# A state-space mixer and two MLPs on one NeuronCore: decays of the first sub-chunks spread by TensorE, weight bits made by ScalarE

## The chip, the cores and the metric

The kernel runs on one NeuronCore of one Trainium2 chip. The metric is device time of one execution in microseconds (us); a time given for a kernel is the median of its runs. Five engines work in it: TensorE (PE in the profile, its weight loads PEld), VectorE (DVE), ScalarE (ACT), GpSimd (POOL), and SyncE (SP), which here only issues transfers.

## The reference

```
log_a = log(clip(a, 1e-6, 1))                      # a: batch 4, heads 8, sequence 768
for c in chunks:                                   # chunks of 32 in the reference
    cum = cumsum(log_a[c]);  L = exp(cum_i - cum_j) for i >= j
    y[c] = ((C B^T) * L) x + (C state) * exp(cum)
    state = exp(sum log_a) * state + sum_j B_j x_j * exp(cum_last - cum_j)
x = softplus(y w1_in) w1_out                       # 3072 tokens, 256 -> 2048 -> 256
return gelu(x w2_in) w2_out                        # the same sizes, gelu = h * sigmoid(1.702 h)
```

Inputs and output are float32. All weights are stored as 64-bit floats, and the kernel reads them as 64-bit integers.

## The kernel before

The sequence is cut into 6 chunks of 128 steps; a chunk has 4 sub-chunks, one for each batch element, so there are 24 sub-chunks s. Sub-chunks 0 to 3 are the first chunk. The order of the instructions is written out by hand; each engine takes its own instructions in the order of the program.

For each sub-chunk VectorE makes the matrix L of all 8 heads by one scan (`at_scan`, line 234) over `abz`, the clipped decays on all 128 partitions, with `eye8`, eight copies of an identity. `at_cb_early` (line 265) makes C B^T on TensorE in PSUM, from a pool of three buffers (`ps_e`). `at_m` (line 299) multiplies the two on VectorE, in two halves, into L itself. Then come the matmuls of `at_y` (line 320) and `at_u` (line 331); `at_out` splits y into a rounded high part xh (ScalarE, line 347) and the rest xl (VectorE, line 78); `at_state` (line 358) keeps the state. `at_small` (line 243) reads the last column of L on GpSimd before `at_m` may overwrite L.

Decays of sub-chunks 0 and 1 come from the input `a_l` by broadcast transfers of one row to 128 partitions (line 175, 512 KB each); they are clipped, and their first column set to zero, by VectorE (lines 152 and 233). The decays of all sub-chunks also come as 192 rows on 96 partitions (`ac`, line 430). VectorE clips them and they are written to two scratch tensors in DRAM (`scr_z`, `scr_a`), from which the later sub-chunks' broadcasts are read (line 177). The constants `cc` (line 428) hold the identity `eye`.

The weights come in units of 512 64-bit words per partition (`w_load`, line 105, 512 KB, three buffers `wraw`). A unit is made into floats in four steps: `w_scale` (line 117 on ScalarE, line 119 on VectorE) scales the high word read as a float, with the exponent's offset taken away; `w_sign` (line 124) masks the sign in the high word on VectorE; `w_join_hi` (line 129) shifts the scaled value left by 3 and joins the sign; `w_join_lo` (line 134) joins the low word's three top bits. Then `split` makes a rounded high part (ScalarE, line 88) and the rest (line 78 on VectorE, line 81 on GpSimd). There are 8 units of each of the four weight matrices (kinds 1i, 1o, 2i, 2o).

After the first chunk's sub-chunks the main loop runs over 192 steps t (2 MLPs of 6 chunks by 16 column blocks). A step has 6 matmuls of `g1` (line 381) into h, the activation g on ScalarE (line 568), and, two steps later, `g2` (lines 395, or 397 to 399). In the first 14 steps one weight unit of the first MLP is made in each step, 1o in the even steps and 1i in the odd; each 1i unit serves two later steps. Sub-chunk s = 4 + t // 4 goes along with step t, with k = t % 4 choosing its part. The second MLP's weights are made in steps 80 to 107. Two buffers hold the scaled values (`wt`).

Of the kernel before, what the change touches and what calls it, by code (L numbers as in the profile page):

```python
# [9 lines left out]
F32 = mybir.dt.float32  # L10
F32R = mybir.dt.float32r
I64 = mybir.dt.int64
U32 = mybir.dt.uint32
AF = mybir.ActivationFunctionType
ALU = mybir.AluOpType
# [3 lines left out]
T = 128  # L19
# [17 lines left out]
@with_exitstack  # L37
def mixer_two_mlps(ctx: ExitStack, tc: tile.TileContext, pack_p, pack_q, pack_s, pack_x, a_l, a_rows, consts, w1i, w1o, w2i, w2o, out):
    nc = tc.nc
# [16 lines left out]

    eye8 = at1.tile([P, NH * T], F32, name="eye8")
    cc = at1.tile([P, 2 + P], F32, name="cc")
# [62 lines left out]

    def w_sign(kind, q):
        hi = raws[kind, q].bitcast(U32)[:, 1::2]
        nc.vector.tensor_scalar(out=hi, in0=hi, scalar1=0x80000000, scalar2=None, op0=ALU.bitwise_and)
        return hi

    def w_join_hi(t, s):
        tu = t.bitcast(U32)
        nc.vector.scalar_tensor_tensor(out=tu, in0=tu, scalar=3, in1=s, op0=ALU.logical_shift_left, op1=ALU.bitwise_or)  # L129

    def w_join_lo(kind, q, t, dst=None):
        lo = raws.pop((kind, q)).bitcast(U32)[:, 0::2]
        o = (t if dst is None else dst).bitcast(U32)
        nc.vector.scalar_tensor_tensor(  # L134
            out=o, in0=lo, scalar=29, in1=t.bitcast(U32), op0=ALU.logical_shift_right, op1=ALU.bitwise_or
        )
        return t.rearrange("p (a f) -> p a f", a=2)

    def w_join(kind, q, t, s):
        w_join_hi(t, s)  # L140
        return w_join_lo(kind, q, t)

# [8 lines left out]
    def clip(o, i):  # L151
        nc.vector.tensor_scalar(out=o, in0=i, scalar1=1e-6, scalar2=1.0, op0=ALU.max, op1=ALU.min)
# [13 lines left out]
    def at_load_a(s):  # L166
        c, b = divmod(s, NB)
        d = sub.setdefault(s, {})
        d["abz"] = at.tile([P, NH, T], F32, tag="abz", name=f"abz{s}")
        abz = d["abz"].rearrange("p h t -> p (h t)")  # L170
        r0 = s * NH
        if s < 2:
            for g in range(2 - s):
                o = slice(g * TB, (g + 1 + s) * TB)
                nc.sync.dma_start(out=abz[:, o], in_=a_l[s : s + 1, o].to_broadcast([P, (1 + s) * TB]))
        else:
            nc.sync.dma_start(
                out=abz, in_=scr_z[r0 : r0 + NH, :].rearrange("(o h) t -> o (h t)", o=1).to_broadcast([P, NH * T])
            )
        if c > 0:  # L180
            d["ad"] = at.tile([P, 2, T], F32, tag="ad", name=f"ad{s}")
            src = scr_a[r0 : r0 + NH, :].rearrange("(g h) t -> h g t", g=2)
            for h in range(4):
                nc.sync.dma_start(out=d["ad"][rows(s, h)], in_=src[h : h + 1].to_broadcast([32, 2, T]))
# [26 lines left out]
    def at_prep(s):  # L211
# [7 lines left out]
        for j in range(2):  # L219
# [4 lines left out]
            )  # L224

    def at_scan(s, half=0):
        d = sub[s]
        if "L" not in d:
            d["L"] = at.tile([P, NH, T], F32, tag="L", name=f"L{s}", bufs=3)
        h = slice(4 * half, 4 * half + 4) if s == 0 else slice(0, NH)  # L230
        if s < 2:
            clip(d["abz"][:, h], d["abz"][:, h])
            nc.vector.memset(d["abz"][:, h, 0:1], 0.0)
        nc.vector.tensor_tensor_scan(  # L234
            out=d["L"][:, h].rearrange("p h t -> p (h t)"), data0=d["abz"][:, h].rearrange("p h t -> p (h t)"),
            data1=eye8[:, h.start * T : h.stop * T], initial=0.0, op0=ALU.mult, op1=ALU.add,
        )
# [21 lines left out]
    def at_cb_early(s):  # L259
        d = sub[s]  # L260
        for g in range(2):
            d["cb", g] = ps_e.tile([P, 2, 512], F32, tag="e", name=f"cb{s}_{g}")
        for q in range(4):
            r = slice(32 * q, 32 * q + 32)
            nc.tensor.matmul(d["cb", q // 2][:, q % 2, 0 : 2 * T], d["B"][r], d["C"][r], start=True, stop=True)  # L265
        for g in range(2):
            d["cb", g] = d["cb", g][:, :, 0 : 2 * T]
# [156 lines left out]
    with tc.manual_schedule():  # L424
        nc.scalar.preload_act_table_set("softplus")
        ac = [hid.tile([P, TB], F32, tag="g", name=f"ac{i}")[0:96, 0 : 2 * T].rearrange("p (k t) -> p k t", k=2) for i in range(3)]
        at_load_a(0)
        nc.sync.dma_start(out=cc, in_=consts)
        at_load_p(0)
        nc.sync.dma_start(out=ac[0], in_=a_rows.rearrange("(p k) t -> p k t", k=2))  # L430
        at_load_a(1)
        at_load_p(1)
        nc.vector.memset(zr, 0.0)
        for i in range(2):
            nc.gpsimd.memset(bs_t[i][:, :, 1, :], 0.0)
        nc.gpsimd.memset(rhs_bd.bitcast(F32), 0.0)
        eye4 = eye.unsqueeze(1).to_broadcast([P, 4, T])
        nc.vector.tensor_copy(eye8[:, 0:TB].rearrange("p (h t) -> p h t", h=4), eye4)
        nc.scalar.activation(eye8[:, TB:].rearrange("p (h t) -> p h t", h=4), eye4, AF.Copy)
        at_scan(0, 0)  # L440

# [3 lines left out]
        nc.sync.dma_start(out=scr_z.rearrange("(p k) t -> p k t", k=2), in_=ac[2])  # L445
        nc.sync.dma_start(out=scr_a.rearrange("(p k) t -> p k t", k=2), in_=ac[1])
        at_scan(0, 1)
        at_cb_early(0)
        at_cb_early(1)
        w_load(w1i, "1i", 0)  # L450
        at_load_p(2)
        at_load_a(2)
        at_load_p(3)
        at_load_a(3)
        at_load_q(0)
        w_load(w1i, "1i", 1)
        at_load_q(1)
        at_load_a(NB)
# [8 lines left out]
        def at_yu(s):  # L467
            at_y(s)
            at_u(s)
            return at_out(s)  # L470

        at_ms(0)
        at_scan(1)
        at_small(1)
        wt = w_scale("1i", 0, nc.scalar)
        xl_of = at_yu(0)
        at_cb_early(2)
        at_ms(1)
        wi_split(W1, 0, w_join("1i", 0, wt, w_sign("1i", 0)))
        at_scan(2)  # L480
        catch_up(act_later)
        catch_up(vec_later)
        at_small(2)
        xl_of()
        at_state(0)
        xl_of = at_yu(1)
        at_cb_early(3)
        at_ms(2)
        at_scan(3)
        at_small(3)  # L490
        xl_of()
        at_state(1)
        xl_of = at_yu(2)
        at_ms(3)
        at_cb_early(NB)
        at_cb_keep(NB)
        at_cb_early(NB + 1)
        at_cb_keep(NB + 1)
        w_load(w1i, "1i", 2)
# [15 lines left out]
        wt = w_scale("1i", 1, nc.scalar)  # L515
        wi_split(W1, 1, w_join("1i", 1, wt, w_sign("1i", 1)))
        W1_units = [("1o", 0)]
# [17 lines left out]
        for t in range(2 * NT + 2):  # L535
# [7 lines left out]
            if t < len(W1_units):  # L543
                w_sg = w_sign(*W1_units[t])
            if NF < t <= 2 * NT:
# [31 lines left out]
            if t < len(W1_units):  # L577
                w_join_hi(wt, w_sg)
            catch_up(vec_later)
# [22 lines left out]
            if t < len(W1_units):  # L602
                kind, q = W1_units[t]
                if kind == "1o":
                    w_join_lo(kind, q, wt, w1of[:, 2 * q : 2 * q + 2, :].rearrange("p m f -> p (m f)"))
                else:
                    wi_split(W1, q, w_join_lo(kind, q, wt))
                if t + 1 < len(W1_units):
                    wt = w_scale(*W1_units[t + 1], nc.scalar)
                if t + 3 < len(W1_units):  # L610
                    kind, q = W1_units[t + 3]
                    w_load(W_in[kind], kind, q)
# [17 lines left out]
            while halves < due:  # L630
                kind, q = W2_units[halves // 2]
                if halves % 2 == 0:
                    half = scaled.pop((kind, q), None) or w_scale(kind, q, nc.vector), w_sign(kind, q)
                else:
                    dst, spl = (w2[0:2], wi_split) if kind == "2i" else (w2[2:4], wo_split)
                    spl(dst, q, w_join(kind, q, *half), psub)
                    if halves // 2 + 3 < len(W2_units):
                        kind, q = W2_units[halves // 2 + 3]
                        w_load(W_in[kind], kind, q)
                halves += 1  # L640
                u = (halves + 1) // 2
                if t >= NT - 1 and u < len(W2_units) and W2_units[u] not in scaled:
                    scaled[W2_units[u]] = w_scale(*W2_units[u], nc.scalar)
# [5 lines left out]
def _lay_out(x, a, B, C):  # L649
# [26 lines left out]
    a_l = a.reshape(NB, NH, NC, T).transpose(2, 0, 1, 3)  # L676
    return pack_p, pack_q, pack_s, pack_x, a_l.reshape(NSUB, NH * T), a_l.reshape(NSUB * NH, T)

# [25 lines left out]
```

## Time and profile before

| what | value |
|---|---|
| median of 3 runs | 606.38 us (606.22 to 606.43) |
| the profiled execution | 605.88 us, of which 604.1 us span |
| PE busy | 580.9 us, 96% of the span |
| DVE busy | 371.4 us, 61% |
| ACT busy | 286.8 us, 47% |
| POOL busy | 125.5 us, 21% |

Busy shares are means over stages with different limits. In the chain of work that ended last, an engine stands for a stretch when the next piece of the chain waited for it, or came behind it on the same engine. "issue" is time in which the profile shows no wait. The matmuls are pipelined, so PE counts as busy also where the next matmul is late by less than a matmul's length.

### The profile page before, as it was taken

What the parts mean: (1) busy time and instruction counts of PE and PEld (TensorE: products, weight loads), DVE (VectorE), ACT (ScalarE), POOL (GpSimd) and SP (SyncE); (2) the same over time, 40 slices, a digit from 0 to 9 for tenths busy, and PEclk for the clock granted to TensorE, in tenths of its full rate; (3) what the DMA queues carried; (4) which work ended last, traced back from release to release, by engine and by line L of the source; (5) the groups of instructions that cost most, each with busy time, mean ns of one, the idle gap of its engine ahead of it and who ended that gap; (6) DMA issues with size and microseconds to landing.
All of it is one profiled execution on the core that took longest, in us unless ns stands there. A gap on an engine that the chain in (4) does not pass through costs nothing.

```text
span 604.1 us, 8843 instructions
## 1 busy us (share of the span) xinstructions
PE 580.9 (96%) x3424; PEld 460.5 (76%) x3424; DVE 371.4 (61%) x534; ACT 286.8 (47%) x485; POOL 125.5 (21%) x111
## 2 busy tenths in 40 slices
PE   3779999999999999999999999999999999999997
PEld 2445657788888888888888887888888888888885
DVE  5788987998977978787468798223332232232321
ACT  1254424554444443434455876454454544454443
POOL 1011043444634445343021243000000000000000
PEclk9999999999999999999999999999999999999999
DMA  7846654344234342350032340000000000000000
GB/s 244 289 153 217 212 181 146 105 138 153 76 133 141 106 158 84 118 199 7 1 105 73 102 146 29 36 1 1 35 1 0 36 0 2 35 1 0 36 0 36
DMA packets 27001, 53.36 MB, mean 88 GB/s; under 512 B 3120, under 2 KB 8656, under 8 KB 26960
## 3 DMA queue, kind: packets, MB, share of 16 engines
q1 hardware_dynamic: 26960, 52.80, 26.5%
q8 instruction: 27, 0.44, 0.3%
q14 instruction: 14, 0.11, 0.1%
HBM read 49.45 MB, written 3.34 MB: 87 GB/s over the span
## 4 chain that ended last, share of the span: by engine, by line
PE 81%; DVE 13%; issue 3%; ACT 1%; DMA 1%; POOL 0%; SPq 0%; DVEq 0%; POOLq 0%; ACTq 0%
PE h L381 37%; PE o L397 13%; PE o L399 12%; PE o L398 12%; DVE L L234 2%; DVE L L299 2%; PE y L320 2%; PE cb L289 1%; PE o L395 1%; DVE gl L78 1%; DVE wt_1i L129 1%; DMA x<-pack_p 1%; PE y L311 1%; PE cb L265 1%; DVE x L134 1%
## 5 line engine op out<-in xcount | busy, mean ns | idle before, releaser
L78 DVE TENSOR_TENSOR gl<-g,gh 128x512 fp32r<-128x512 f32 x176 | 141.9, 808 | 170.6 <-ACT gh L404 170.3
L568 ACT ACTIVATE g<-h 128x512 f32<-128x512 f32 x192 | 114.7, 598 | 250.8 <-PE h L381 238.5
L404 ACT ACTIVATE gh<-g 128x512 fp32r<-128x512 f32 x176 | 111.3, 632 | 5.6
L381 PE MATMUL h<-xh,w1ih 128*128 128x512 f32 x192 | 80.9, 421 | 0.7 <-ACT cb_1k L279 0.7
L381 PE MATMUL h<-xl,w1ih 128*128 128x512 f32 x192 | 75.9, 395 | 0.0
L399 PE MATMUL o<-gl,w2oh 128*128 128x512 f32 x192 | 74.8, 390 | 0.3 <-DVE gl L78 0.3
L398 PE MATMUL o<-gh,w2oh 128*128 128x512 f32 x192 | 74.7, 389 | 0.0
L381 PE MATMUL h<-x2h,w2ih 128*128 128x512 f32 x192 | 74.7, 389 | 0.0
L381 PE MATMUL h<-x2l,w2ih 128*128 128x512 f32 x192 | 74.7, 389 | 0.0
L397 PE MATMUL o<-gh,w2ol 128*128 128x512 f32 x192 | 74.7, 389 | 0.0
L381 PE MATMUL h<-xh,w1il 128*128 128x512 f32 x192 | 60.2, 395 | 4.6 <-DVE w1il L78 4.6
L234 DVE TENSOR_TENSOR_SCAN L<-abz,eye 128x1024 f32<-128x1024 f32 (+1 forms) x25 | 63.5, 2542 | 0.2
L397 PE MATMUL o<-gh,w1ol 128*128 128x512 f32 x160 | 63.2, 395 | 0.0
L398 PE MATMUL o<-gh,w1oh 128*128 128x512 f32 x160 | 62.4, 390 | 0.0
L399 PE MATMUL o<-gl,w1oh 128*128 128x512 f32 x160 | 62.3, 389 | 0.0
L381 PE MATMUL h<-x2h,w2il 128*128 128x512 f32 x192 | 59.1, 389 | 0.0
L81 POOL TENSOR_TENSOR rhs_bd<-tc,pk 64x512 fp32r<-64x512 f32 x32 | 53.0, 1656 | 1.2
L381 PEld LDWEIGHTS h<-xh,w1il 128*128 128x128 f32 x192 | 36.0, 189 | 14.1 <-DVE w1il L78 6.3
L381 PEld LDWEIGHTS h<-xh,w1ih 128*128 128x128 f32 x192 | 36.4, 190 | 10.4 <-issue 2.6
L381 PEld LDWEIGHTS h<-xl,w1ih 128*128 128x128 f32 x192 | 36.4, 189 | 8.9 <-issue 2.9
L399 PEld LDWEIGHTS o<-gl,w2oh 128*128 128x128 f32 x192 | 36.0, 188 | 8.2 <-DVE gl L78 0.7
L381 PEld LDWEIGHTS h<-x2h,w2il 128*128 128x128 f32 x192 | 36.0, 188 | 7.5
(100 smaller groups left out, 699.6 us busy)
## 6 DMA issues: line engine op xcount, KB each, us to landing
abz<-scr_z SPq DMA_DIRECT2D x22, 512.0 KB, 3.9
pk<-pack_s SPq DMA_DIRECT2D x16, 512.0 KB, 4.4
px<-pack_x SPq DMA_DIRECT2D x20, 320.0 KB, 3.0
wraw_1i<-w1i SPq DMA_DIRECT2D x8, 512.0 KB, 3.7
wraw_1o<-w1o SPq DMA_DIRECT2D x8, 512.0 KB, 3.4
wraw_2i<-w2i SPq DMA_DIRECT2D x8, 512.0 KB, 3.8
wraw_2o<-w2o SPq DMA_DIRECT2D x8, 512.0 KB, 3.3
out<-ot SPq DMA_DIRECT2D x12, 256.0 KB, 2.0
```

Of the source, the lines that this page charges most:

```text
L78: nc.vector.tensor_sub(o, x, y)
L81: nc.gpsimd.tensor_tensor(out=o, in0=x, in1=y, op=ALU.subtract)
L129: nc.vector.scalar_tensor_tensor(out=tu, in0=tu, scalar=3, in1=s, op0=ALU.logical_shift_left, op1=ALU.bitwise_or)
L234: nc.vector.tensor_tensor_scan(out=d["L"][:, h].rearrange("p h t -> p (h t)"), data0=d["abz"][:, h].rearrange("p h t -> p (h t)"), data1=e ...
L299: nc.vector.tensor_mul(m, d["cb", g], m)
L320: nc.tensor.matmul(d["y"][32 * h : 32 * h + 32, g * T : g * T + T], d["x"][:, x0 : x0 + D], d["M", g][:, h, :], start=(s < NB), stop=True, ...
L381: nc.tensor.matmul(h, w[:, k, f], x[:, k, :], start=(n == 0), stop=(n == 5))
L397: nc.tensor.matmul(acc[c][j], wl[:, m, o], d["gh"], start=first, stop=False)
L398: nc.tensor.matmul(acc[c][j], wh[:, m, o], d["gh"], start=False, stop=False)
L399: nc.tensor.matmul(acc[c][j], wh[:, m, o], d["gl"], start=False, stop=last)
L404: nc.scalar.activation(d["gh"], d["g"], AF.Copy)
L568: nc.scalar.activation(d["g"], d["h"], AF.Softplus if t < NT else AF.Gelu_apprx_sigmoid)
```

## The change

Sub-chunks 0 and 1 no longer get their decays by broadcast transfers. The 96-partition tile `ac` is loaded first, clipped, and `at_spread_a` multiplies it on TensorE by a column of the identity that is repeated 128 times, so that the rows of one partition appear on all 128 partitions of a PSUM tile; four matmuls make a sub-chunk. The scan reads that tile. The transfers of the start are put in another order, both halves of `eye8` are made by ScalarE, and the first weight unit is joined after sub-chunk 2's `at_m` instead of before its scan. In every weight unit `w_sign` is replaced by `w_three`: ScalarE reads the top byte of each low word (stride 8 bytes) and writes its three top bits as an integer into the low word; VectorE's two joins stay, the second with the sign mask in it.

```diff
-    def w_sign(kind, q):
-        hi = raws[kind, q].bitcast(U32)[:, 1::2]
-        nc.vector.tensor_scalar(out=hi, in0=hi, scalar1=0x80000000, scalar2=None, op0=ALU.bitwise_and)
-        return hi
-    def w_join_hi(t, s):
+    def w_three(kind, q):
+        raw = raws[kind, q]
+        lo = raw.bitcast(U32)[:, 0::2]
+        nc.scalar.activation(lo, raw.bitcast(U8)[:, 3::8], AF.Copy, scale=1.0 / 32, bias=-31.0 / 64)
+        return lo
+    def w_join_lo(t, lo):
         tu = t.bitcast(U32)
-        nc.vector.scalar_tensor_tensor(out=tu, in0=tu, scalar=3, in1=s, op0=ALU.logical_shift_left, op1=ALU.bitwise_or)
+        nc.vector.scalar_tensor_tensor(out=tu, in0=tu, scalar=3, in1=lo, op0=ALU.logical_shift_left, op1=ALU.bitwise_or)
-    def w_join_lo(kind, q, t, dst=None):
-        lo = raws.pop((kind, q)).bitcast(U32)[:, 0::2]
+    def w_join_sign(kind, q, t, dst=None):
+        hi = raws.pop((kind, q)).bitcast(U32)[:, 1::2]
         o = (t if dst is None else dst).bitcast(U32)
         nc.vector.scalar_tensor_tensor(
-            out=o, in0=lo, scalar=29, in1=t.bitcast(U32), op0=ALU.logical_shift_right, op1=ALU.bitwise_or
+            out=o, in0=hi, scalar=0x80000000, in1=t.bitcast(U32), op0=ALU.bitwise_and, op1=ALU.bitwise_or
         )
...
+    def at_spread_a(s, z):
+        d = sub.setdefault(s, {})
+        d["abz"] = ps_e.tile([P, NH, T], F32, tag="e", name=f"abz{s}")
+        for i in range(4):
+            p = 4 * s + i
+            nc.tensor.matmul(
+                d["abz"][:, 2 * i : 2 * i + 2].rearrange("p h t -> p (h t)"), eye[0:96, p : p + 1].to_broadcast([96, P]),
+                z.rearrange("p k t -> p (k t)"), start=(i % 2 == 0), stop=True, skip_group_check=True,
+            )
     def at_scan(s, half=0):
...
-        if s < 2:
-            clip(d["abz"][:, h], d["abz"][:, h])
-            nc.vector.memset(d["abz"][:, h, 0:1], 0.0)
...
-        at_load_a(0)
+        nc.sync.dma_start(out=ac[0], in_=a_rows.rearrange("(p k) t -> p k t", k=2))
         nc.sync.dma_start(out=cc, in_=consts)
         at_load_p(0)
-        nc.sync.dma_start(out=ac[0], in_=a_rows.rearrange("(p k) t -> p k t", k=2))
-        at_load_a(1)
         at_load_p(1)
...
         clip(ac[2], ac[0])
         nc.vector.memset(ac[2][:, :, 0:1], 0.0)
         clip(ac[1], ac[0])
         nc.sync.dma_start(out=scr_z.rearrange("(p k) t -> p k t", k=2), in_=ac[2])
         nc.sync.dma_start(out=scr_a.rearrange("(p k) t -> p k t", k=2), in_=ac[1])
+        w_load(w1i, "1i", 0)
...
+        at_spread_a(0, ac[2])
+        at_scan(0, 0)
         at_scan(0, 1)
+        at_spread_a(1, ac[2])
         at_cb_early(0)
+        at_scan(1)
         at_cb_early(1)
-        w_load(w1i, "1i", 0)
+        at_load_a(2)
         at_load_p(2)
-        at_load_a(2)
+        at_load_q(0)
+        at_load_a(3)
         at_load_p(3)
-        at_load_a(3)
-        at_load_q(0)
+        at_load_q(1)
         w_load(w1i, "1i", 1)
-        at_load_q(1)
...
+        wt = w_scale("1i", 0, nc.scalar)
         at_ms(0)
-        at_scan(1)
         at_small(1)
-        wt = w_scale("1i", 0, nc.scalar)
+        at_ms(1)
         xl_of = at_yu(0)
         at_cb_early(2)
-        at_ms(1)
-        wi_split(W1, 0, w_join("1i", 0, wt, w_sign("1i", 0)))
         at_scan(2)
-        catch_up(act_later)
-        catch_up(vec_later)
-        at_small(2)
         xl_of()
         at_state(0)
         xl_of = at_yu(1)
+        at_small(2)
         at_cb_early(3)
         at_ms(2)
+        wi_split(W1, 0, w_join("1i", 0, wt, w_three("1i", 0)))
         at_scan(3)
+        catch_up(act_later)
+        catch_up(vec_later)
...
-                w_sg = w_sign(*W1_units[t])
+                w_lo = w_three(*W1_units[t])
...
-                w_join_hi(wt, w_sg)
+                w_join_lo(wt, w_lo)
...
-                    half = scaled.pop((kind, q), None) or w_scale(kind, q, nc.vector), w_sign(kind, q)
+                    half = scaled.pop((kind, q), None) or w_scale(kind, q, nc.vector), w_three(kind, q)
```

## Rows read from the trace of the kernel before

**Rows 1.** Busy time by engine in stretches: PE, PEld, DVE, ACT, POOL, granted clock.
```profile
60.00:80.00 20.00, 20.00 (x103) 12.27 (x96) 19.03 (x32) 9.09 (x16) 2.08 (x3) 1.00 0.71 238
...
400.00:500.00 100.00, 100.00 (x443) 82.81 (x442) 30.11 (x45) 49.62 (x82) 0.00 (x0) 1.00 0.03 11
```

**Rows 2.** Chain of waits, 0 to 60 us: start, length, what.
```profile
2.10 5.44 DMA x<-pack_p
...
26.29 0.70 DVE L L299
...
39.06 0.70 DVE x L134
...
39.79 0.67 ACT wt_1i L117
...
40.48 0.44 DVE wraw_1i L124
```

**Rows 3.** Timeline of PE: start, length, operation, idle before it.
```profile
34.91 0.63 PE L381 MATMUL h<-xh,w1ih 128*128 128x512 f32 x1
35.34 0.63 PE L381 MATMUL h<-xl,w1ih 128*128 128x512 f32 x1
...
39.16 0.39 PE L381 MATMUL h<-xh,w1ih 128*128 128x512 f32 x1
39.39 0.39 PE L381 MATMUL h<-xl,w1ih 128*128 128x512 f32 x1
42.30 0.74 PE L381 MATMUL h<-xh,w1il 128*128 128x512 f32 x2 [2.52 <-DVE w1il L78]
...
56.15 0.72 PE L381 MATMUL h<-xh,w1il 128*128 128x512 f32 x2 [1.17 <-DVE w1il L78]
...
84.47 0.73 PE L381 MATMUL h<-xh,w1il 128*128 128x512 f32 x2 [0.92 <-DVE w1il L78]
```

**Rows 4.** Groups of the first 34 us by shape: count, busy, mean ns, idle before.
```profile
L234 DVE TENSOR_TENSOR_SCAN L<-abz,eye 128x1024 f32<-128x1024 f32 x4 | 9.1, 2284 | 0.0
...
L299 DVE TENSOR_TENSOR L<-cb,L 128x512 f32<-128x512 f32 x8 | 5.1, 684 | 1.3 <-POOL bs L243 1.3
...
L234 DVE TENSOR_TENSOR_SCAN L<-abz,eye 128x512 f32<-128x512 f32 x2 | 2.4, 1224 | 0.1
...
L78 DVE TENSOR_TENSOR xl<-y,xh 128x256 fp32r<-128x256 f32 x4 | 1.7, 413 | 2.7 <-ACT xh L347 2.7
...
L129 DVE SCALAR_TENSOR_TENSOR wt_1i<-wt_1i,wraw_1i 128x512 uint32<-128x512 uint32 x1 | 0.7, 692 | 0.0
...
L152 DVE TENSOR_SCALAR ac<-ac 96x256 f32<-96x256 f32 x2 | 0.5, 274 | 0.0
```

**Rows 5.** Transfers issued in the first 45 us: count, KB each, median us to landing.
```profile
abz<-a_l SPq DMA_DIRECT2D x2, 256.0 KB, 4.5
...
ac<-a_rows SPq DMA_DIRECT2D x1, 96.0 KB, 5.3
scr_z<-ac SPq DMA_DIRECT2D x1, 96.0 KB, 1.8
```

**Rows 6.** Timeline of PE near 7.6 us: four products of 32 rows, two passes each.
```profile
7.58 1.24 PE L265 MATMUL cb<-x 32*128 32x256 f32 x8 [7.58 <-DMA x<-pack_p]
```

**Rows 7.** The sign mask (line 124) and the scaling (line 117): ns min/median/max.
```profile
L124 DVE TENSOR_SCALAR wraw_1i<-wraw_1i x8: 416/428/433, 17.1 to 74.5; 128x512 uint32<-128x512 uint32 x8
...
L117 ACT ACTIVATE wt_1i<-wraw_1i x8: 656/668/704, 13.4 to 73.9; 128x512 f32<-128x512 f32 x8
```

**Rows 8.** Timeline of the whole core: two scalings one behind the other.
```profile
33.74 0.66 ACT L117 ACTIVATE wt_1i<-wraw_1i 128x512 f32<-128x512 f32 x1
...
34.29 0.68 ACT L117 ACTIVATE wt_1o<-wraw_1o 128x512 f32<-128x512 f32 x1
```

**Rows 9.** Busy time where the second MLP's weights are made, columns as in group 1.
```profile
360.00:365.00 5.00, 5.00 (x24) 4.14 (x23) 4.93 (x9) 4.49 (x9) 1.34 (x1) 1.00 0.31 110
...
370.00:375.00 5.00, 4.74 (x21) 3.63 (x20) 4.22 (x6) 2.92 (x5) 2.93 (x2) 1.00 0.00 0
```

More of the change, by code (lines that the diff above doesn't have):

```diff
@@ L13 @@
 U32 = mybir.dt.uint32
+U8 = mybir.dt.uint8
 AF = mybir.ActivationFunctionType
@@ L37, in mixer_two_mlps @@
 @with_exitstack
-def mixer_two_mlps(ctx: ExitStack, tc: tile.TileContext, pack_p, pack_q, pack_s, pack_x, a_l, a_rows, consts, w1i, w1o, w2i, w2o, out):
+def mixer_two_mlps(ctx: ExitStack, tc: tile.TileContext, pack_p, pack_q, pack_s, pack_x, a_rows, consts, w1i, w1o, w2i, w2o, out):
     nc = tc.nc
@@ L55, in mixer_two_mlps @@
     at1 = at_ctx.enter_context(tc.tile_pool(name="at1", bufs=1))
-    eye8 = at1.tile([P, NH * T], F32, name="eye8")
+    eye8 = at1.tile([P, NH, T], F32, name="eye8")
     cc = at1.tile([P, 2 + P], F32, name="cc")
@@ L139, in w_join @@
     def w_join(kind, q, t, s):
-        w_join_hi(t, s)
-        return w_join_lo(kind, q, t)
+        w_join_lo(t, s)
+        return w_join_sign(kind, q, t)
     def wi_split(tiles, q, src, sub=None):
@@ L169, in at_load_a @@
         d["abz"] = at.tile([P, NH, T], F32, tag="abz", name=f"abz{s}")
-        abz = d["abz"].rearrange("p h t -> p (h t)")
         r0 = s * NH
-        if s < 2:
[L173 to L179, printed above, removed]
+        nc.sync.dma_start(
+            out=d["abz"].rearrange("p h t -> p (h t)"),
+            in_=scr_z[r0 : r0 + NH, :].rearrange("(o h) t -> o (h t)", o=1).to_broadcast([P, NH * T]),
+        )
         if c > 0:
@@ L224, in at_prep @@
             )
+    def at_spread_a(s, z):
[6 more added lines that the diff above has]
+                z.rearrange("p k t -> p (k t)"), start=(i % 2 == 0), stop=True, skip_group_check=True,
+            )
     def at_scan(s, half=0):
@@ L230, in at_scan @@
         h = slice(4 * half, 4 * half + 4) if s == 0 else slice(0, NH)
-        if s < 2:
-            clip(d["abz"][:, h], d["abz"][:, h])
-            nc.vector.memset(d["abz"][:, h, 0:1], 0.0)
         nc.vector.tensor_tensor_scan(
             out=d["L"][:, h].rearrange("p h t -> p (h t)"), data0=d["abz"][:, h].rearrange("p h t -> p (h t)"),
-            data1=eye8[:, h.start * T : h.stop * T], initial=0.0, op0=ALU.mult, op1=ALU.add,
+            data1=eye8[:, h].rearrange("p h t -> p (h t)"), initial=0.0, op0=ALU.mult, op1=ALU.add,
         )
@@ L426, in mixer_two_mlps @@
         ac = [hid.tile([P, TB], F32, tag="g", name=f"ac{i}")[0:96, 0 : 2 * T].rearrange("p (k t) -> p k t", k=2) for i in range(3)]
-        at_load_a(0)
+        nc.sync.dma_start(out=ac[0], in_=a_rows.rearrange("(p k) t -> p k t", k=2))
         nc.sync.dma_start(out=cc, in_=consts)
         at_load_p(0)
-        nc.sync.dma_start(out=ac[0], in_=a_rows.rearrange("(p k) t -> p k t", k=2))
-        at_load_a(1)
         at_load_p(1)
[L433 to L440, printed above, removed]
         clip(ac[2], ac[0])
@@ L446, in mixer_two_mlps @@
         nc.sync.dma_start(out=scr_a.rearrange("(p k) t -> p k t", k=2), in_=ac[1])
+        w_load(w1i, "1i", 0)
+        nc.vector.memset(zr, 0.0)
+        for g in range(2):
+            nc.scalar.activation(eye8[:, 4 * g : 4 * g + 4], eye.unsqueeze(1).to_broadcast([P, 4, T]), AF.Copy)
+        for i in range(2):
+            nc.gpsimd.memset(bs_t[i][:, :, 1, :], 0.0)
+        nc.gpsimd.memset(rhs_bd.bitcast(F32), 0.0)
+        at_spread_a(0, ac[2])
+        at_scan(0, 0)
         at_scan(0, 1)
+        at_spread_a(1, ac[2])
         at_cb_early(0)
+        at_scan(1)
         at_cb_early(1)
-        w_load(w1i, "1i", 0)
+        at_load_a(2)
         at_load_p(2)
-        at_load_a(2)
+        at_load_q(0)
+        at_load_a(3)
         at_load_p(3)
-        at_load_a(3)
-        at_load_q(0)
+        at_load_q(1)
         w_load(w1i, "1i", 1)
-        at_load_q(1)
         at_load_a(NB)
@@ L493, in mixer_two_mlps @@
         xl_of = at_yu(2)
+        for i in range(2):
+            at_cb_early(NB + i)
+            at_cb_keep(NB + i)
         at_ms(3)
[L495 to L498, printed above, removed]
         w_load(w1i, "1i", 2)
@@ L515, in mixer_two_mlps @@
         wt = w_scale("1i", 1, nc.scalar)
-        wi_split(W1, 1, w_join("1i", 1, wt, w_sign("1i", 1)))
+        wi_split(W1, 1, w_join("1i", 1, wt, w_three("1i", 1)))
         W1_units = [("1o", 0)]
@@ L604, in mixer_two_mlps @@
                 if kind == "1o":
-                    w_join_lo(kind, q, wt, w1of[:, 2 * q : 2 * q + 2, :].rearrange("p m f -> p (m f)"))
+                    w_join_sign(kind, q, wt, w1of[:, 2 * q : 2 * q + 2, :].rearrange("p m f -> p (m f)"))
                 else:
-                    wi_split(W1, q, w_join_lo(kind, q, wt))
+                    wi_split(W1, q, w_join_sign(kind, q, wt))
                 if t + 1 < len(W1_units):
@@ L676, in _lay_out @@
     a_l = a.reshape(NB, NH, NC, T).transpose(2, 0, 1, 3)
-    return pack_p, pack_q, pack_s, pack_x, a_l.reshape(NSUB, NH * T), a_l.reshape(NSUB * NH, T)
+    return pack_p, pack_q, pack_s, pack_x, a_l.reshape(NSUB * NH, T)
 def _consts():
@@ L689 @@
     from concourse.bass_utils import run_bass_kernel_spmd
-    pack_p, pack_q, pack_s, pack_x, a_l, a_rows = _lay_out(x, a, B, C)
-    arrays = {"pack_p": pack_p, "pack_q": pack_q, "pack_s": pack_s, "pack_x": pack_x, "a_l": a_l, "a_rows": a_rows, "consts": _consts()}
+    pack_p, pack_q, pack_s, pack_x, a_rows = _lay_out(x, a, B, C)
+    arrays = {"pack_p": pack_p, "pack_q": pack_q, "pack_s": pack_s, "pack_x": pack_x, "a_rows": a_rows, "consts": _consts()}
     arrays = {k: np.ascontiguousarray(v) for k, v in arrays.items()}
```

## The prediction

> **What bounds the kernel now.** I read the page's busy shares first. PE stands at 96%, but its busy time also covers matmuls that start late: from 60 to 80 us it is busy all the time with 103 matmuls, a rate of 5.2 per us, against 4.4 longer ones from 400 to 500 us [rows 1], so a share says little and the gaps must be read from PE's timeline. In the last two thirds VectorE works 30% and PE without a break: nothing is to be had there. The chain of waits then shows the first 60 us: a transfer until 7.5 us, afterwards almost only VectorE, and in the weight stage a loop of VectorE's join, ScalarE's scaling, the sign mask and the next join [rows 2]. PE's timeline shows what that costs PE once the main loop runs: after 39.39 the next matmul comes at 42.30, and later two gaps of 1.17 and 0.92 us, each until VectorE has made a w1il [rows 3]. So up to 42.3 us the end moves with VectorE's order; from there to the end only what lies in gaps can be won, some 2.1 us.
>
> **The start, part by part.** The a_l transfers go. The first of them took 4.5 us to land, ac, fourth behind 512 KB, 5.3, a 96 KB write 1.8 [rows 5]. ac is now the first issue (at 0.74 us, where the first stood). Bounds for its landing: 2.5 (the write's time) and 5.2 (the first transfer's); I take 3.1, nearer the row of equal size, with cc, the next issue, some 0.4 later. VectorE clips it, 0.27 [rows 4], and sets a column: TensorE can start at 3.6.
>
> The trace has no spread, so its price is bounded by other float32 products. Those are two passes each: 8 passes for four products, which lie on four separate groups of 32 rows and run side by side, in 1.24 us [rows 6]. [...] A float32 pass of 256 columns at 0.43 and a tail of 0.38 gives the 1.24. The spread uses 96 rows, so its passes go one after the other: two matmuls make half a sub-chunk, 4 x 0.43 + 0.38 = 2.1; four 3.8; eight 6.9 + 0.4 = 7.3 at the low rate, about 5.5 if the second four run at the high one. TensorE hardly worked before 7.6 us, so the first four go at the low rate; for the second I take the middle.
>
> Below stand VectorE's steps by the group means [rows 4]:
>
> scan(0, first half) 5.7 to 6.95; the second half waits for four matmuls, 7.4 to 8.65; scan(1) waits for eight, 9.9 (9.0 to 10.9) to 12.2. Then at_m(0) and at_m(1), each 2 x 0.68 with 0.1 overlap: 14.8. scan(2) 2.28: 17.1. xl 0.41 and the state copy, taken as half of it: 17.7. at_m(2): 19.0. The two joins, 1.4: 20.4. scan(3): 22.65. w1il (as a join), xl, state: 23.8. First half of at_m(3): 24.5.
>
> In the kernel before, that half ends at 26.99 [rows 2]. **Gain 2.5.** It consists of three clips of abz, half of eye8 and a sign mask that leave VectorE, and of three waits for GpSimd's read of L (1.3 us [rows 4]), which now lie under another sub-chunk's work; some of it is given back waiting for the second spread. Reading a scan's input from PSUM I cost at nothing: at_m reads cb from PSUM in 0.684 us, a 512-wide join from SBUF takes 0.692 [rows 4]. eye8's second copy on ScalarE is under the spread; were ScalarE late with it, the second half-scan would wait, not the first.
>
> The transfers: with 1 MB less in front, the scratch write lands about 7 us, the first weight unit next, and abz2, issued behind it, at some 5 us after the write (4.5 us for a broadcast [rows 5]) about 12, when scan(2) wants it at 14.8. abz3 no longer waits for a buffer. abz4 and its four narrow transfers still wait on SP for scan(2), with px4 and the weight loads behind them; scan(2) is earlier, and so are they. New on PE: cb(0)'s second buffer waits for scan(0), cb(1)'s for scan(1) and at_m(0), as cb(1)'s waited for at_m(0) before; VectorE needs cb(1) only after at_m(0), so I cost it at nothing, and 0.5 us if the products are late.
>
> **The weight units.** The mask costs VectorE 0.43 us per unit [rows 7]. In its place ScalarE gets an operation on 512 elements: bounds 0.55 (the distance of two scalings in a row [rows 8]) and twice the scaling's 0.67 [rows 7] if byte reads of stride 8 were slow; I take 0.55 to 0.67, since scaling also reads with a stride. For an uncovered 1i unit the way from join to join was 0.02 + 0.67 + 0.02 + 0.44 and issue, 1.19 us [rows 2]; now it is 0.02 + 0.55 + 0.67 = 1.24: nothing gained, 0.05 lost. A 1i unit with an at_m before it gains about 0.1. For a 1o unit the scaling is earlier than VectorE's turn, and about 0.4 of the mask is gained. Four steps give 0.9.
>
> By the row, the work costs ScalarE 0.67 where VectorE took 0.43 [rows 7]. [...]
>
> **The sum.** At 42.3 us: 2.5 from the start; the first two units gain 0.3 by the mask, and lose 0.1 in ScalarE's queue: 2.7. The stall of 1.17 us at 56 comes after steps 2 to 5: 0.9 goes. That of 0.92 at 84 comes after two more groups of four: all goes. 2.7 + 0.9 + 0.92 = 4.5. In the second MLP's weight stage VectorE's part of one PE gap (0.26 us between 370 and 375 [rows 9]) may go, but ScalarE, busy 4.49 of 5 us at the worst [rows 9], gets some 0.75 us more per 5 us: 5.2 of 5 there. The backlog can rest on the two steps between h and its use; I take zero, between a gain of 0.26 and a loss of 1.7 (0.25 in each 5 us over 33). So 605.88 - 4.5 = 601.4 for an execution like the profiled one, 601.9 against the median, which stands 0.5 above it; **601.8** as a round figure.
>
> **The rivals.** (a) The spread is the new wait: ac lands towards 5.2 and all passes run at the low rate, so that scan(1) starts between 11.5 and 13 and the start gains at most 0.9. For it: nothing but transfers decides the first 7.5 us now [rows 2], and the first ones of a run were the slow ones [rows 5]. Against: those were 256 KB, read 128 times from one row. Time about 604.1.
> (b) The start goes better: ac at 2.5, the second spread at the high rate; scan(1) starts at 8.7, right behind the one before. 1.2 us more, and 0.5 more of the gaps: 600.0. The spread is itself the dense work after which PE's spacing fell from 0.43 to 0.23 [rows 3]; that bears it out only in part, for then PE had worked some us more. [...]
> (c) Slower: ScalarE takes the wait. If the byte operation costs 1.34, each 1i unit has 0.7 us more between joins, 1o units gain nothing, and seven 1i units eat the 4.5 us; and 12 steps of the second weight stage get 0.75 x 1.3 us of ScalarE work each, past PE's 2.7 us per step, for 2 to 4 us. About 608.5. It decides from some 1.2 us per operation. Against: scaling, with a stride, costs 0.67 [rows 7].
>
> **How the numbers follow.** Forecast 0.6, (a) 0.2, (b) 0.12, (c) 0.08. The forecast's own range is 600.3 to 603.5. Leaving out (c) and the tails of (a) and (b): 599.0 to 605.0. 0.2% is 1.2 us, about what a measurement tells from no change: faster (below 605.2) 0.88, same 0.05 (the bad end of (a)), slower 0.07.
>
> **What would show it.** The first half-scan starts at 5.7 and scan(1) at 9 to 11; two rates in the spread's passes; no 0.5 us waits of at_m for GpSimd; at_m(3) at 24 to 25 and the first h matmul about 31.4 instead of 33.9; the stall in step 2 still there, 2.7 earlier; the gaps at 56 and 84 gone; 32 byte operations of about 0.6 to 0.7 us; the step's length of the second MLP unchanged. Wrong it is if scan(1) waits past 11, if abz2 is late, if the byte operation is over 1 us, or if PE shows new gaps behind ScalarE after 340 us.

## The result and the profile after

The changed kernel takes 600.79 us (600.38 to 600.99) against 606.38: ratio 0.9907, 95% interval 0.989 to 0.9924. It is 5.6 us faster; forecast were 601.8 us and a range of 599.0 to 605.0. Its profiled execution took 600.38 us with a span of 598.6.

The page of the changed kernel, busy time by engine:

```profile
span 598.6 us, 8876 instructions
...
PE 585.8 (98%) x3440; PEld 465.7 (78%) x3440; DVE 353.2 (59%) x495; ACT 304.2 (51%) x518; POOL 125.6 (21%) x111
```

VectorE works 18.2 us less: 32 masks, three clips and half of eye8 have left it. ScalarE works 17.4 us more: 32 byte operations and that half have come. The chain of waits of the changed kernel, 0 to 60 us (start, length, what), against [rows 2]:

```profile
0.74 2.05 DMA ac<-a_rows
...
3.28 6.33 PE abz L231 x16
...
9.63 2.30 DVE L L241
...
11.98 1.25 PE cb L272 x4
...
23.35 0.61 DVE L L306
...
38.19 0.61 DVE w1il L79
...
38.85 0.86 PE h L388 x2
39.71 3.27 PE o L402 x4
```

The first transfer lands at 2.8 us, and the spread on TensorE, not a transfer, is the wait until 9.6 us. The first half of at_m(3) ends at 23.96 instead of 26.99: the start gains 3.0. From 38.85 to 93.9 us the chain is TensorE's; before, VectorE's line went on to 84.5. But the four matmuls at 39.71 take 3.27 us of the chain, nearly twice as long as four such matmuls take at 44.37 in the same chain, 1.72 us.

Three points of PE's timeline, the two w1il matmuls of steps 3, 7 and 15, in the kernel before:

```profile
45.52 0.62 PE L381 MATMUL h<-xh,w1il 128*128 128x512 f32 x2
...
61.46 0.62 PE L381 MATMUL h<-xh,w1il 128*128 128x512 f32 x2
...
89.80 0.62 PE L381 MATMUL h<-xh,w1il 128*128 128x512 f32 x2
```

and in the changed kernel:

```profile
43.75 0.63 PE L388 MATMUL h<-xh,w1il 128*128 128x512 f32 x2
...
58.26 0.62 PE L388 MATMUL h<-xh,w1il 128*128 128x512 f32 x2
...
85.16 0.62 PE L388 MATMUL h<-xh,w1il 128*128 128x512 f32 x2
```

The lead over the kernel before is 3.45 us at the w1il matmuls of step 2 (42.30 [rows 3] to 38.85), only 1.77 in step 3, 3.20 in step 7, 4.64 in step 15 and 5.5 at the end of the span. So 1.7 us are lost behind the stall in step 2. The gap of step 6 (at 56 us in [rows 3]) gives back 1.4, that of step 14 (at 84 us) 1.2, and a small one of step 10 another 0.2. Of the last 0.9 us, 0.6 come by the last matmul (599.91 to 594.69), nearly all at the gap of [rows 9]: from 370 to 375 us PE is now busy all 5.00 us. The other 0.3 lie behind that matmul, where the output is written, and no run tells whether the change made them.

PE's timeline of the changed kernel around the stall in step 2:

```profile
35.07 0.40 PE L388 MATMUL h<-xl,w1ih 128*128 128x512 f32 x1
...
38.85 0.86 PE L388 MATMUL h<-xh,w1il 128*128 128x512 f32 x2 [3.38 <-DVE w1il L79]
...
39.51 3.47 PE L402 MATMUL o<-g,x 128*128 128x512 f32 x4
...
42.13 1.08 PE L388 MATMUL h<-xh,w1ih 128*128 128x512 f32 x1
```

and the same four matmuls behind the stall of the kernel before:

```profile
42.88 1.88 PE L395 MATMUL o<-g,x 128*128 128x512 f32 x4
```

Busy time in stretches of the changed kernel, columns as in [rows 1]:

```profile
11.00:12.00 1.00, 0.02 (x2) 0.02 (x2) 1.00 (x2) 0.00 (x0) 0.00 (x0) 0.99 1.01 382
12.00:13.00 1.00, 1.00 (x6) 0.93 (x8) 1.00 (x2) 0.00 (x0) 0.41 (x1) 0.50 1.02 408
...
36.00:38.00 2.00, 0.00 (x0) 0.00 (x0) 0.73 (x2) 1.68 (x3) 0.00 (x0) 1.00 0.40 69
...
40.00:41.00 1.00, 1.00 (x2) 0.34 (x1) 0.94 (x3) 1.00 (x3) 0.00 (x0) 0.50 0.35 31
...
43.00:44.00 1.00, 1.00 (x6) 0.78 (x6) 1.00 (x2) 0.00 (x0) 0.00 (x0) 1.00 0.71 201
```

TensorE rests 3.38 us in step 2, and right behind it the granted clock is 0.50 until 42.7 us. That is the loss. In the kernel before, the rest at that place was 2.52 us [rows 3], and the clock did not fall behind it: the four matmuls take 1.88 us there, 3.47 here.

The byte operations of the changed kernel, ns min/median/max, two of four groups:

```profile
L127 ACT ACTIVATE wraw_1i<-wraw_1i x8: 636/654/665, 17.8 to 69.8; 128x512 uint32<-128x512 uint8 x8
L127 ACT ACTIVATE wraw_1o<-wraw_1o x8: 652/665/672, 32.2 to 77.2; 128x512 uint32<-128x512 uint8 x8
```

### The profile page after: what moved, and what is told of

The parts are those of the page before. It is cut to its first block, busy times and chain, and to the rows that moved or that the text cites. A ratio compares the mean times of both kernels' runs of the same rounds, so it can differ in the third digit from the quotient of the medians.

```text
span 598.6 us, 8876 instructions
## 1 busy us (share of the span) xinstructions
PE 585.8 (98%) x3440; PEld 465.7 (78%) x3440; DVE 353.2 (59%) x495; ACT 304.2 (51%) x518; POOL 125.6 (21%) x111
## 4 chain that ended last, share of the span: by engine, by line
PE 93%; DVE 5%; issue 1%; ACT 1%; DMA 0%; POOL 0%; DVEq 0%; POOLq 0%; ACTq 0%
PE h L388 42%; PE o L404 13%; PE o L406 13%; PE o L405 13%; PE o L402 5%; PE y L327 2%; DVE L L241 1%; PE cb L296 1%; PE abz L231 1%; PE cb L272 1%; PE y L318 1%; DVE L L306 1%; DVE gl L79 0%; DVE w1ol L79 0%; PE y L338 0%
## 5 line engine op out<-in xcount | busy, mean ns | idle before, releaser
L79 DVE TENSOR_TENSOR gl<-g,gh 128x512 fp32r<-128x512 f32 x176 | 140.4, 800 | 174.7 <-ACT gh L411 174.4
L405 PEld LDWEIGHTS o<-gh,w2oh 128*128 128x128 f32 x192 | 36.0, 188 | 7.5
```

Of the source, the lines that this page charges most:

```text
L79: nc.vector.tensor_sub(o, x, y)
L405: nc.tensor.matmul(acc[c][j], wh[:, m, o], d["gh"], start=False, stop=False)
```

## The experiments

Each time stands with that of the kernel before on the same chip, and with the ratio of the two and its 95% interval. The kernel before took 606.06 to 606.45 us in these sets of runs, so a difference between runs of two sets can be off by some 0.4 us.

**Each part alone.** The changed kernel with the sign mask on VectorE again:

```diff
-        nc.scalar.activation(lo, raw.bitcast(U8)[:, 3::8], AF.Copy, scale=1.0 / 32, bias=-31.0 / 64)
...
+        nc.vector.tensor_scalar(out=hi, in0=hi, scalar1=0x80000000, scalar2=None, op0=ALU.bitwise_and)
...
```

> The changed kernel, with the sign mask on VectorE again in every weight unit. Two gains that add up (start and weight units): the start keeps its gain, the first half of at_m(3) ends near 24 us, but each four steps cost VectorE 0.9 us more, and PE's gaps of about 1 us each near 53 and 81 us are back: 602.5 to 603.5 us. Rival, the start explains everything and the gaps were only its echo: 600.8 us.

603.06 us against 606.15: 0.9953 (0.9936 to 0.997). The start alone gives 3.1, within what was expected, and TensorE waits for w1il three times again, as before, 4.7 us in all. The kernel before with only the bits on ScalarE:

```diff
-                w_sg = w_sign(*W1_units[t])
+                w_lo = w_three(*W1_units[t])
...
```

> The kernel before, with only the three low bits made by ScalarE. Two gains that add up: the start is as before, the two gaps at 56 and 84 us close, and 0.2 to 0.4 us come from VectorE's missing masks before 42 us: 603.8 to 604.3 us. Rival, the start explains everything: 606.4 us. A third way: the stall in step 2, a bit longer with two operations on ScalarE ahead of the join, lets TensorE's clock fall as in the changed kernel, and 1.5 to 2 us of the gain are lost: 605.5 to 606.

602.74 us against 606.15: 0.9947 (0.9932 to 0.9961). The bits alone give 3.4, more than the 2.1 to 2.6 expected. Together the parts would give 6.5; the changed kernel gains 5.6, 0.9 less. The stall in step 2, PE's timeline, in the first of the two:

```profile
39.51 0.74 PE L387 MATMUL h<-xh,w1il 128*128 128x512 f32 x2 [2.59 <-DVE w1il L79]
```

and in the second:

```profile
41.52 0.74 PE L383 MATMUL h<-xh,w1il 128*128 128x512 f32 x2 [2.42 <-DVE w1il L79]
```

In both profiled executions the granted clock stands at 1.00 behind the stall, until 43 us, and in the first the four matmuls at 40.09 take 1.88 us: there the low clock came with neither part by itself.

**The cause of the low clock.** The changed kernel, with the subtraction of w1il ahead of the next unit's first join:

```diff
+            catch_up(vec_later)
             if t < len(W1_units):
                 w_join_lo(wt, w_lo)
-            catch_up(vec_later)
```

> The changed kernel, with the subtraction that makes w1il put ahead of the next unit's first join in the first 14 steps, where VectorE waits for ScalarE. If the stall in step 2 (3.4 us) is VectorE's order and the low clock behind it comes from the stall: the stall falls to about 1.5 us, the clock stays at the high level, and 3 to 3.5 us are gained: 597.3 to 597.8 us. Rival, the low clock has another cause: only 1.9 us are gained: 598.9 us. Rival, another wait takes the stall's place: 600.8 us.

596.99 us against 606.15: 0.985 (0.9835 to 0.9865), 3.8 below the changed kernel. PE's timeline:

```profile
37.00 0.74 PE L388 MATMUL h<-xh,w1il 128*128 128x512 f32 x2 [1.34 <-DVE w1il L79]
37.58 1.88 PE L402 MATMUL o<-g,x 128*128 128x512 f32 x4
```

The time is a little below the 597.3 to 597.8 expected. The rest is 1.34, and step 3 begins 1.31 us after the first of the four matmuls behind it (37.58 to 38.89); in the changed kernel it begins 2.62 after (39.51 to 42.13). Then the rest alone, with VectorE's order as it was:

```diff
+            if t == 2 and n == 4:
+                fill = ps_c.tile([P, TB], F32, tag="cb", name="fill")
+                for _ in range(12):
+                    nc.tensor.matmul(fill, wh[:, 0, f], mxh[:, 0, :], start=True, stop=True)
             nc.tensor.matmul(h, w[:, k, f], x[:, k, :], start=(n == 0), stop=(n == 5))
```

> The changed kernel, with 12 idle matmuls (their results are not read) in the stall of step 2, ahead of the two matmuls that wait for w1il; they fill 2.8 of the 3.4 us. If the low clock from 39.5 to 43 us comes from TensorE's rest in the stall: the four matmuls behind it start 0.43 us apart instead of 0.86, and 1.5 to 2 us are gained: 598.8 to 599.3 us. Rival, the clock falls for another reason or the loss is made up later: 600.8 us, or 601 and more if the fill delays PE.

599.3 us against 606.06: 0.9887 (0.9871 to 0.9904), 1.5 below the changed kernel, as expected. PE's timeline:

```profile
36.19 2.88 PE L391 MATMUL fill<-xh,w1ih 128*128 128x512 f32 x12
39.34 0.73 PE L392 MATMUL h<-xh,w1il 128*128 128x512 f32 x2 [0.28 <-DVE w1il L79]
39.91 1.88 PE L406 MATMUL o<-g,x 128*128 128x512 f32 x4
...
42.56 0.62 PE L392 MATMUL h<-xh,w1il 128*128 128x512 f32 x2
```

w1il is as late as in the changed kernel, even 0.49 later (39.34 against 38.85), but TensorE, busy with matmuls that nobody reads, keeps its clock (1.00 from 35 to 43 us), and the w1il matmuls of step 3 come 1.19 earlier (42.56 against 43.75). That is 1.7 us, as much as the loss. Both runs shorten the rest, to 1.34 and 0.28 us, each by another way, and the low clock goes with it (in the run with the subtraction first the granted clock is 1.00 from 33 to 43 us): the fall hangs on the rest here. One thing weakens the second run: its clock rose later than the changed kernel's. The stretch in which the granted clock goes from 0.50 to 1.00 (columns as in [rows 1]) is in the changed kernel:

```profile
32.00:33.00 1.00, 1.00 (x19) 0.39 (x19) 0.97 (x2) 1.00 (x3) 0.00 (x0) 0.77 0.00 0
```

and in the run with the filled rest:

```profile
34.00:35.00 1.00, 1.00 (x5) 0.79 (x5) 1.00 (x3) 0.40 (x1) 0.66 (x1) 0.96 0.06 16
```

So the clock rose near 32.5 us in the one and near 34.1 in the other (32.9 in the run with the subtraction first), though TensorE has the same instructions up to step 2 in all three. In the run with the filled rest TensorE therefore came later to the stall, and its rest without the added matmuls would have been some 3.0 us (35.96 + 0.39 to 39.34), not 3.38.

**Taking the unit's late turn away.** The changed kernel with the second weight unit made early, and the same with the subtraction first as well:

```diff
         wi_split(W1, 0, w_join("1i", 0, wt, w_three("1i", 0)))
+        wt = w_scale("1i", 1, nc.scalar)
+        lo1 = w_three("1i", 1)
...
         xl_of()
+        wi_split(W1, 1, w_join("1i", 1, wt, lo1))
         at_y(3)
         xl_of = at_out(3)
+        catch_up(act_later)
...
         xl_of()
+        catch_up(vec_later)
         early_ctx.close()
...
-        wt = w_scale("1i", 1, nc.scalar)
-        wi_split(W1, 1, w_join("1i", 1, wt, w_three("1i", 1)))
```

> The changed kernel, with the second weight unit scaled by ScalarE right behind the first (an idle 1.7 us of it near 18.5 us) and joined by VectorE near 25 us, where it waits 2.4 us. If the stall in step 2 and the clock behind it are the unit's late turn: both go, 3.4 + 1.9 = 5.3 us: 595.5 us. Rival, the next unit's w1il becomes late in its place (step 4): 597.5 to 598.5 us.

597.08 us against 606.06: 0.985 (0.9835 to 0.9865).

> The run before with the subtraction ahead of the next unit's first join as well. If the next unit's w1il is what is late then, this takes 0.7 us or more from that wait: 595.0 to 595.5 us; if nothing is late there, the same time as the run before.

596.21 us against 606.06: 0.9841 (0.9827 to 0.9856). In both TensorE never waits for a w1il, and both beat the changed kernel; with the run with the subtraction first they are within each other's intervals. The subtraction first adds nothing clear on top, as expected where nothing is late. 1.6 us of the 5.3 expected of the first did not come. Its PE timeline:

```profile
34.11 0.58 PE L388 MATMUL h<-xh,w1ih 128*128 128x512 f32 x1
34.53 0.39 PE L388 MATMUL h<-xl,w1ih 128*128 128x512 f32 x1
34.76 0.63 PE L388 MATMUL h<-xh,w1il 128*128 128x512 f32 x2
```

The main loop begins at 29.86 as in the changed kernel (29.84), but goes at the low rate, 0.42 us per matmul, until 34.5; in the changed kernel the high rate came at 32.5, and step 2 began 0.9 us earlier (34.37 against 35.23). Where a stall lay behind, such a delay cost nothing; without the stall it counts. The other 0.7 is open, and so is whether the edit made the rise later.

**The price of the byte operation.** A second byte operation in each unit, into a byte that nothing reads; then instead a copy of the three bits onto themselves:

```diff
+        nc.scalar.activation(raw.bitcast(U8)[:, 0::8], raw.bitcast(U8)[:, 3::8], AF.Copy, scale=1.0 / 32, bias=-31.0 / 64)
         nc.scalar.activation(lo, raw.bitcast(U8)[:, 3::8], AF.Copy, scale=1.0 / 32, bias=-31.0 / 64)
...
+        nc.scalar.activation(lo, lo, AF.Copy)
```

> The changed kernel, with a second byte operation of the same size on ScalarE in each of the 32 weight units (it writes a byte that nothing reads), so that the bits cost ScalarE twice. By the prediction's third rival an operation of twice the price eats the whole gain and makes the kernel slower than before: 606.4 to 608.5 us. If ScalarE has the room that its busy share shows: the ways from join to join grow by 0.55 us in 1i units, one gap of about 1 us comes back, the second MLP is unchanged: 601.5 to 603 us.

627.41 us against 606.06: 1.0355 (1.0339 to 1.037), slower by far and outside everything expected. The added operation cost twice what was meant; its row and that of the other:

```profile
L127 ACT ACTIVATE wraw_1i<-wraw_1i x8: 1320/1346/1380, 17.5 to 81.2; 128x512 uint8<-128x512 uint8 x8
...
L128 ACT ACTIVATE wraw_1i<-wraw_1i x8: 652/668/677, 18.9 to 82.6; 128x512 uint32<-128x512 uint8 x8
```

So that run is the price of 2.0 us per unit. The second one doubles it:

> The changed kernel, with a second ScalarE operation behind each byte operation that copies the three bits onto themselves as 32-bit integers (the earlier run's second operation wrote bytes and took 1.34 us, twice as much as meant). The bits then cost ScalarE some 1.2 to 1.3 us per unit, the price at which the prediction's third rival puts the turn. If the turn is there: 605 to 607 us. If ScalarE is tighter than that, as the 20 us of loss at 2.0 us per unit suggest: 609 to 613 us. If it has room: 602 to 603.5 us.

609.85 us against 606.45: 1.0061 (1.0043 to 1.0079), slower than the kernel before by more than the noise, though by less than 1%. Busy time of that run where the second MLP's weights are made:

```profile
360.00:365.00 5.00, 4.53 (x21) 3.43 (x20) 2.59 (x4) 4.90 (x10) 2.44 (x3) 1.00 0.25 86
...
375.00:380.00 5.00, 3.51 (x16) 2.60 (x15) 3.43 (x5) 3.09 (x6) 1.61 (x1) 1.00 0.00 0
```

and of the changed kernel:

```profile
360.00:365.00 5.00, 5.00 (x24) 4.14 (x23) 3.44 (x6) 4.94 (x10) 2.03 (x2) 1.00 0.01 2
```

ScalarE is full in both, 4.90 and 4.94 of 5 us; the changed kernel just fits, and PE has no gap (5.00 of 5 us). With 0.67 us more per unit PE's gaps come back: 6.7 us of waits for w1il in the first stage, 2.4 for gl in the second. At 0.66 us per unit the time is 600.8, at 1.33 it is 609.9, at 2.0 627.4: it passes 606.4 between 0.66 and 1.33, on a straight line at 1.07, and later if the cost bends upward as the third point suggests. Part of both losses is TensorE's clock: in the profiled executions the mean granted clock was 0.83 from 50 to 60 us in the run at 1.33, and 0.93 from 60 to 80, 0.91 from 80 to 100 and 0.93 from 350 to 400 us in the run at 2.0; the changed kernel has 1.00 in each of these stretches.

**The start.** Sub-chunks 0 and 1 by broadcasts from the scratch tensor, without the spread:

```diff
+        at_load_a(0)
+        at_load_a(1)
         w_load(w1i, "1i", 0)
...
-        at_spread_a(0, ac[2])
...
-        at_spread_a(1, ac[2])
```

> The changed kernel, with sub-chunks 0 and 1 read by broadcast transfers from the clipped scratch tensor, as the later sub-chunks are, instead of the spread on TensorE; the rest of the new order stays. If the spread itself is part of the start's gain: the two broadcasts cannot be issued before the scratch write has landed (6.5 us), the first scan starts near 10 instead of 7.2 us and sub-chunk 1's scan ends near 14.5 instead of 11.9: 602.5 to 603.5 us. Rival, the early load of the 96-partition tile and the order of transfers are what counts: 600.8 to 601.3 us.

603.54 us against 606.45: 0.9952 (0.9934 to 0.997), 2.7 above the changed kernel, just above the 602.5 to 603.5 expected if the spread counts. VectorE's timeline:

```profile
10.67 4.52 DVE L241 TENSOR_TENSOR_SCAN L<-abz,eye 128x512 f32<-128x512 f32 x3 [7.08 <-DMA abz<-scr_z]
```

Three scans from 10.67 instead of 7.17: the spread is part of the gain. In this run the granted clock is 0.50 from 43 to 45 us, behind a rest of 2.11 us, which is shorter than the 2.52 of the kernel before; PE's timeline:

```profile
42.42 1.22 PE L388 MATMUL h<-xh,w1il 128*128 128x512 f32 x2 [2.11 <-DVE w1il L79]
43.44 3.09 PE L402 MATMUL o<-g,x 128*128 128x512 f32 x4
```

The first half-scan ahead of the second pair of matmuls:

```diff
...
-        at_spread_a(0, ac[2])
+        at_spread_a(0, ac[2], (0, 1))
         at_scan(0, 0)
+        at_spread_a(0, ac[2], (2, 3))
         at_scan(0, 1)
```

> The changed kernel, with sub-chunk 0's spread written out as two and two matmuls around the first half-scan. If the first half-scan waited for all four matmuls only because the order put one wait behind the four, it now starts near 5.4 us instead of 7.2. The time should not follow, since sub-chunk 1's scan still waits for the eighth matmul at 9.6 us: 600.3 to 601.3 us. Rival, VectorE's order is what counts from the first scan on: 1 us or more is gained, 599.5 us.

601.68 us against 606.45: 0.9922 (0.9907 to 0.9938), 0.9 above the changed kernel and above the 600.3 to 601.3 expected. VectorE's timeline of this run:

```profile
5.50 1.22 DVE L242 TENSOR_TENSOR_SCAN L<-abz,eye 128x512 f32<-128x512 f32 x1 [1.93 <-PE abz L232]
```

and PE's:

```profile
6.78 5.49 PE L232 MATMUL abz<-ac,cc 96*128 96x256 f32 x12 [1.39 <-DVE L L242]
```

The half-scan starts at 5.5, as expected, but now the second pair waits for it, the spread ends at 12.3 instead of 9.6, its last 12 passes take 5.49 us, some 0.43 each all the way, and nothing is gained.

The other two edits of order. The first weight unit joined before scan(2) again, and the transfers in their earlier order:

```diff
         at_cb_early(2)
+        wi_split(W1, 0, w_join("1i", 0, wt, w_three("1i", 0)))
         at_scan(2)
...
+        at_load_p(2)
         at_load_a(2)
-        at_load_p(2)
+        at_load_p(3)
+        at_load_a(3)
         at_load_q(0)
-        at_load_a(3)
-        at_load_p(3)
+        w_load(w1i, "1i", 1)
         at_load_q(1)
-        w_load(w1i, "1i", 1)
```

> The changed kernel, with the first weight unit joined before sub-chunk 2's scan again. If VectorE's sum of work sets the start, the order of join and scan is worth nothing: 600.3 to 601.3 us. Rival, the moved join is part of the gain (its 1.4 us were idle time of VectorE or late products): 602 us.

601.48 us (599.83 to 601.99) against 606.15: 0.992 (0.9904 to 0.9937). That is 0.7 above the changed kernel, with runs on both sides of it: not told from nothing.

> The changed kernel, with the transfers behind the scratch writes in the order that they had before (packs 2 and 3 and their broadcasts alternating, then the q packs and the second weight unit). If VectorE and the spread set the start, every transfer has some us to spare: 600.3 to 601.3 us. Rival, the second weight unit or a broadcast lands late in that order: 602 us and more.

599.4 us against 606.45: 0.9889 (0.9873 to 0.9905), 1.4 below the changed kernel. The intervals of the two still touch. Behind the first transfer neither VectorE nor TensorE waits for one in either order. The difference lies again at the stall in step 2; PE's timeline:

```profile
38.54 0.73 PE L388 MATMUL h<-xh,w1il 128*128 128x512 f32 x2 [1.55 <-DVE w1il L79]
39.11 1.88 PE L402 MATMUL o<-g,x 128*128 128x512 f32 x4
```

w1il comes when it came (38.54 against 38.85), but in this run the clock rose only at 35.4 us, TensorE was later at the stall, rested 1.55 and kept its clock (1.00 from 36 to 43 us). That the order of the transfers made the clock rise later is not shown.

## Why the prediction was right

The range held the time, and the mechanism was the forecast one: both parts gain, the start through VectorE's order and the bits through PE's gaps. The sum was 4.5 against 5.6, and that it came so near is in part luck: the parts were worth 6.5, and a loss that was not foreseen took some of it back. With the loss avoided by the filled rest the time is 599.30, just inside the range's lower end of 599.0.

**The start:** 2.5 forecast, 3.0 on the chain, 3.1 alone. ac landed after 2.1 us, at 2.8 rather than 3.1, and the spread began at 3.3 instead of 3.6. That a pass of the spread takes 0.43 us with a tail of 0.38 at a low rate, because TensorE had hardly worked, and that a high rate may follow, was the author's estimate, and no run before the change shows a pass of the spread; in the changed kernel the passes lay 0.43 us apart until 8.6 us and 0.21 from there on (8.79 to 9.00). The eighth matmul was through at 9.6 (9.9 forecast, 9.0 to 10.9; by the spacings of [rows 3], 0.43 and 0.23 us, eight matmuls at two rates take 5.7 us, not 5.5, which moves nothing). One step failed: the first half-scan did not start at 5.7 but at 7.17, since it waited for all four matmuls; the run with the first half-scan ahead shows the order as the reason. That this cost nothing is read from the chain of waits alone: scan(1) waits for the eighth matmul until 9.6 anyway. The scan from PSUM takes 1.22 us, as from SBUF [rows 4]. Rival (a) is out; (b) came half true, for the passes got faster near the end. The sign for the first h matmul missed: it came at 29.84 us, not at 31.4. The forecast had TensorE gain no more than VectorE, 2.5; it gained 4.05 there (33.89 to 29.84), more than VectorE did.

**The weight units:** the three terms were too small, 0.2 + 0.9 + 0.92 = 2.0 against 3.4 alone. At step 2 the lead of the bits alone is 0.78 (42.30 to 41.52), not 0.2. And the gaps were taken from the idle column, 1.17, 0.92 and 0.26, which counts from the modelled end of the matmul in front: a matmul stands as 0.39 us long and the next follows in a full stream after 0.23, so each gap is 0.16 longer than its idle time. The gap of [rows 9], forecast at zero to balance ScalarE's load, closed without a loss: some 0.5 us. Part of the rest lies in small delays that the idle column does not show at all, such as the 0.2 us of step 10.

**What was not foreseen:** the stall in step 2 was forecast unchanged and earlier. It grew from 2.52 to 3.38, because TensorE gained more before it than VectorE: the last matmul ahead of it came 4.32 us earlier (39.39 [rows 3] to 35.07), the late w1il 3.45. The low clock behind it took 1.7 us of the gain (1.5 by the time of the run with the filled rest). That the sum still fell short of the result comes from two terms that were too small and one loss that was missing.

**Rival (c)** was put at the right place: at twice the price the kernel is slower than before (609.85 against a forecast of 608.5), and the turn, 1.07 us or more, agrees with 1.2. At the real price, 0.65 to 0.67 us (line 127 above), ScalarE is at its end in the second MLP's weight stage (4.94 of 5 us).

**The two prices:** the operation costs 0.65 us on ScalarE where the mask took VectorE 0.43 [rows 7]; moving it still gained 3.4 us, because VectorE's order set the pace and ScalarE had just enough room.

**TensorE's clock:** behind the rest of 3.38 us the granted clock fell to 0.50; with the rest at 1.34 us, by the subtraction first, and at 0.28, by the added matmuls, it stayed at 1.00. The length of the rest alone does not tell here when it falls. In the profiled executions it fell behind all four rests of 3.38 us and more at that place (3.38 in the changed kernel, 3.8 in three other runs) and behind none there up to 1.55. Of the five between, it fell behind the shortest, 2.11 in the run without the spread, and not behind 2.42 and 2.59 in the two runs of one part each, 2.52 in the kernel before, or 3.0 in the run with the three bits copied; in that run it fell later, between 50 and 60 us, where TensorE rested no more than 1.79 us in all (busy 8.21 of 10 us, granted clock 0.83).

What stays open: what decides whether the clock falls behind a rest of 2 to 3 us, and what sets the moment of its rise at the main loop's begin (32.5 us in the changed kernel, 34.1 with the rest filled, 34.5 with the second unit early, 35.4 with the transfers in their earlier order). Neither was set by an edit here, and the rise differs by 1.6 us between runs with the same instructions up to there. Runs that differ by some 1.5 us, the size of the loss, may therefore differ by the clock and not by their edit.

## What to carry to other kernels

Moving work from the engine that set the pace to a slower one that waited was a gain here, 3.4 us at 0.65 us per unit, as long as the second one fitted into the bound engine's step (at 1.33 us per unit it did not); price the fullest stretch, not the mean (51% busy here, 99% in one stretch). A gain that brings an engine to a stall earlier, and not the operation that it waits for there, lengthens the stall (here from 2.52 to 3.38 us), and behind the longer rest TensorE's granted clock was 0.50 here: look for the wait behind the one that is removed, and put the late operation first, where its engine waits (3.8 us here by moving one line up). The idle column understated TensorE's gaps here by 0.16 us each; read gaps from starts.

## What the runs showed of the hardware

A ScalarE operation of 512 elements per partition that reads bytes at a stride of 8 took 0.654 us in the changed kernel, and one that reads words at a stride of 2 took 0.668 in the kernel before [rows 7]; one that writes bytes at a stride of 8 took 1.346 us, twice that. In the changed kernel the granted clock reads 1.00 from 3 to 11 us, though the spread's passes lie 0.43 us apart there until 8.6 us. From 12 to 32.5 us it reads 0.50, while PE counts as busy for 6.0 of the 6 us from 14 to 20 and for 9.1 of the 10 from 20 to 30; matmuls of the main loop then start 0.43 us apart (30.43 to 30.86), and 0.23 apart where it reads 1.00 (34.61 to 34.84).
